# A new start for a one-core adaLN, attention and SwiGLU kernel: transfers in program order, TensorE on constants at first, eight heads of q without the shift of h

## The chip, the cores and the metric

The kernel runs on one core of a Trainium2 chip. The metric is device time in microseconds (us), lower is better. Each number is the median of several executions.

## The reference, cut to what matters

```python
mod = silu(c) @ w_mod                       # six vectors of 1024: sa, ca, ga, sb, cb, gb
h = layernorm(x) * (1 + ca) + sa            # x: 2048 rows of 1024
q = h @ wq                                  # 32 heads of 128
p = softmax(q @ k.T / sqrt(128))            # the last 512 keys; 4 key heads, each for 8 query heads
x = x + ga * ((p @ v) @ wo)
h = layernorm(x) * (1 + cb) + sb
x = x + gb * ((silu(h @ w_gate) * (h @ w_up)) @ w_down)     # 3584 wide
```

All inputs are bf16. For the change one identity matters: q = (n·(1+ca)) @ wq + sa @ wq, with n the normalised x. The second term is one column of 128 values per head, the same for every row of x.

## The kernel before

Rows go in four blocks of 512. Attention is a loop of 128 steps, one head of one block per step; q runs three heads ahead. Then comes the feed-forward part. Every weight comes through one transfer queue (SyncE's), and a scheduler decides the order of instructions on each engine. The parts that the change touches, cut:

```python
for tt in range(QT): load_x(tt)
for half in range(DH):
    load_wm(1, half); load_wm(0, half)      # w_mod columns: ca, then sa, 1 MB each
    load_wq(0, 0, (half,))
... # kT by transposing transfer, v, wq of heads 4-7
for half in range(DH):                      # start of the first block
    mod_cols(1, half, ca1, True)            # 32 matmuls of one column each
    mod_cols(0, half, sa, False)
    for dt in range(4 * half, 4 * half + 4):
        ln_affine(("h1", 0), dt, h0_ps[half][:, dt % 4, :], ca1, sa, dt % 2 == 0)
    ... # q of three heads, half of the sum
at(g + 2, load_rb, g); at(g + 4, emit_norm, g)      # softmax sums of four heads, back from DRAM
at(max(0, 4*hg - 3 + 2*i + j), bound_wq, hg, i, j)  # squares of wq for a bound: 32 x 1.23 us of DVE
for k in range(NU + 1):                             # the loop over heads
    if k % 4 == 2 and k + 6 < NU: load_wq((k + 6) // H, ((k + 6) % H) // 4)
    if k < NU: emit_s(k)                            # scores, exp, sums
    if k + LEAD < NU: emit_q(k + LEAD)              # LEAD = 3
    run_tasks(k)
    if k >= 1: ... emit_o(k - 1)
```

## Time and profile before

| | before |
|---|---|
| time, median of 4 executions | 1294.5 us |
| span of the profiled execution | 1293.1 us |
| TensorE (PE) busy | 99% |
| useful matmul time, counted as below | 1253.7 us |
| lost | 39.4 us |

The Trainium skill ("Trainium Kernel Development and Optimization", Performance Expectations) calls matmul busy time "a bad metric" for the distance to the best, because matmuls are pipelined. PE is 99% busy, and that hides where the time went. I therefore count weight loads (PEld), one for each matmul. Each load of a 128x512 matmul that has started counts 216 ns (215.8 unrounded), the spacing of such matmuls in the trace; narrower ones count in proportion; the l_ps and row_ps matmuls, of which four run side by side, count a quarter. Transposes, modulation, bias and warm-up matmuls count nothing. The loss at a time t is t less what was counted by then.

The table of windows of the kernel before (stretch, its length, then busy us and instructions of each engine, granted clock as a share, mean busy share of the transfer engines, GB/s):

```profile
core 0: us, PE busy (x) PEld busy (x) DVE busy (x) ACT busy (x) POOL busy (x), PEclk, DMA share, GB/s
10.00:20.00 10.00, 9.26 (x103) 5.90 (x104) 3.57 (x12) 3.18 (x5) 0.00 (x0) 1.00 1.17 378
20.00:30.00 10.00, 9.25 (x88) 4.60 (x87) 4.31 (x12) 2.77 (x4) 0.00 (x0) 0.83 1.02 254
40.00:60.00 20.00, 20.00 (x109) 8.48 (x108) 20.00 (x37) 14.55 (x21) 0.00 (x0) 1.00 0.71 221
60.00:80.00 20.00, 18.58 (x87) 7.79 (x86) 20.00 (x64) 14.29 (x20) 0.00 (x0) 1.00 1.02 300
80.00:100.00 20.00, 20.00 (x108) 8.64 (x106) 20.00 (x36) 8.13 (x12) 0.00 (x0) 1.00 1.00 334
```

The start is full of transfers (378 GB/s from 10 to 20 us). From 40 to 100 us the vector engine (DVE) is busy all the time, and between 60 and 80 us PE got only 87 matmuls. The timeline of PE at the start and around 77 us (start, length, engine, line, operation, tiles, count; in brackets the idle time before and what ended it):

```profile
15.44 2.72 PE L878 MATMUL q_ps<-hT,wq 128*128 128x512 bf16 x6 [0.44 <-ACT hT L826]
20.19 0.87 PE L728 MATMUL mod_ps<-siluc,wm_1_117 128*128 128x1 bf16 x29
21.31 0.94 PE L728 MATMUL mod_ps<-siluc,wm_1_119 128*128 128x1 bf16 x32 [0.25 <-DVE modT L730]
22.50 1.23 PE L953 MATMUL q_ps<-hT,wq 128*128 128x512 bf16 x4 [0.25 <-DVE modT L730]
23.53 4.27 PE L878 MATMUL q_ps<-hT,wq 128*128 128x512 bf16 x12
...
75.13 0.38 PE L983 MATMUL l_ps<-psB,ones_bf 128*32 128x512 bf16 x1 [0.91 <-DVE psB L975]
76.12 2.38 DVE L1004 TENSOR_TENSOR oT<-oT,rb 128x1024 bf16<-128x1024 bf16 x2
77.42 0.61 PE L1031 MATMUL a_ps<-wo,oT 128*128 128x512 bf16 x2 [0.51 <-DVE oT L1004]
```

Six q matmuls took 2.72 us, twelve took 4.27 us: most of these stood 427 ns apart, half rate. (The window of 10 to 20 us shows a clock of 1.00 all the same: the trace's first clock record starts at 19.8 us, and the view counts time without a record as full.) The clock fell again at 23.2 us. At 75 to 78 us PE waits for DVE.

### The profile page before, as it was taken

Reading aid. Unit: us, or ns where it says so; the run is one execution under the profiler, and the core shown is the slowest. Engines: PE = TensorE matmul, PEld = TensorE weight load, DVE = VectorE, ACT = ScalarE, POOL = GpSimd, SP = SyncE. Lnnn points to the kernel's source line nnn. Section 1 sums busy time; section 2 is a strip of 40 time slices with the busy share of each in tenths; the row PEclk is TensorE's granted clock in tenths of the full one; section 3 lists DMA queues with packets and bytes.
Section 4 is the critical chain, followed back from the end, with each engine's and each line's share of the span. In section 5 each row is a group of like instructions: output and inputs, shape, how many; then the busy total and the mean of one; then the engine's idle time right before and its main releaser. Section 6 shows DMA issues by size and latency. Waiting matters only on the chain.

```text
span 1293.1 us, 15465 instructions
## 1 busy us (share of the span) xinstructions
PE 1274.6 (99%) x6169; PEld 575.1 (44%) x6169; DVE 653.4 (51%) x1144; ACT 454.0 (35%) x646; POOL 0.7 (0%) x6
## 2 busy tenths in 40 slices
PE   6999999999999999999999999999999999999998
PEld 3444444444444444444444444444444444444444
DVE  5999768975569655597654641221222211222122
ACT  3755545655455555555453441001100111011100
POOL 0000000000000000000000000000000000000000
PEclk9999999999999999999999999999999999999999
DMA  9897584665354645355447475453536445454402
GB/s 303 273 320 215 206 203 144 187 172 177 122 184 137 180 139 172 130 156 171 163 137 232 161 224 180 145 191 131 165 105 215 167 144 180 137 191 131 147 18 83
DMA packets 219939, 221.08 MB, mean 171 GB/s; under 512 B 45385, under 2 KB 205129, under 8 KB 219858
## 3 DMA queue, kind: packets, MB, share of 16 engines
q1 hardware_dynamic: 214690, 215.54, 52.6%
q10 hardware_dynamic: 5168, 4.46, 1.0%
q8 instruction: 50, 0.82, 0.2%
q14 instruction: 31, 0.25, 0.1%
HBM read 207.63 MB, written 4.47 MB: 164 GB/s over the span
## 4 chain that ended last, share of the span: by engine, by line
PE 93%; DVE 4%; DMA 1%; issue 1%; ACT 0%; SPq 0%; DVEq 0%
PE gu_ps L1099 30%; PE a_ps L1031 17%; PE d_ps L1119 15%; PE q_ps L953 15%; PE o_ps L1014 8%; PE s_ps L966 7%; DVE junk L893 1%; PE l_ps L983 1%; PE q_ps L878 1%; DVE psA L973 1%; DVE qT L855 1%; DMA rb<-r_d 1%; DVE st L793 0%; DMA hT<-xn 0%; DVE psB L975 0%
## 5 line engine op out<-in xcount | busy, mean ns | idle before, releaser
L968 ACT ACTIVATE pT<-s_ps 128x1024 bf16<-128x1024 f32 x256 | 249.0, 1028 | 8.7 <-PE s_ps L966 5.3
L1031 PE MATMUL a_ps<-wo,oT 128*128 128x512 bf16 x1024 | 242.3, 379 | 1.7 <-DVE qT L855 1.2
L953 PE MATMUL q_ps<-hT,wq 128*128 128x512 bf16 x1000 | 237.1, 380 | 0.3 <-DVE modT L730 0.3
L1104 ACT ACTIVATE sg<-gu_ps 128x512 bf16<-128x512 f32 x112 | 66.9, 597 | 460.4 <-PE gu_ps L1099 306.6
L1105 DVE TENSOR_TENSOR guT<-gu_ps,sg 128x512 bf16<-128x512 f32 x112 | 77.5, 692 | 280.8 <-ACT sg L1104 280.8
L1099 PE MATMUL gu_ps<-hT,wu 128*128 128x512 bf16 x896 | 211.8, 379 | 0.0
L1099 PE MATMUL gu_ps<-hT,wg 128*128 128x512 bf16 x896 | 211.7, 379 | 0.0
L1119 PE MATMUL d_ps<-wd,guT 128*128 128x512 bf16 (+2 forms) x952 | 194.2, 367 | 0.0
L1031 PEld LDWEIGHTS <-oT 128*128 128x128 bf16 x1024 | 99.6, 98 | 123.8 <-issue 2.8
L1016 ACT CAST oT<-o_ps 128x512 bf16<-128x512 f32 x128 | 74.3, 580 | 226.3 <-PE o_ps L1014 226.3
L953 PEld LDWEIGHTS <-wq 128*128 128x128 bf16 x1000 | 97.6, 98 | 118.3 <-issue 0.3
L1119 PEld LDWEIGHTS <-guT 128*128 128x128 bf16 x952 | 90.7, 98 | 103.1
L1099 PEld LDWEIGHTS <-wg 128*128 128x128 bf16 x896 | 87.5, 98 | 105.8
L1099 PEld LDWEIGHTS <-wu 128*128 128x128 bf16 x896 | 87.4, 98 | 106.0 <-DMA wu<-in_B_w_up_dram 0.4
L966 PE MATMUL s_ps<-qT,kT 128*128 128x512 bf16 x512 | 131.8, 379 | 0.6 <-ACT pT L968 0.6
L1014 PE MATMUL o_ps<-pT,v_sb 128*128 128x512 bf16 x512 | 131.8, 380 | 0.0
L973 DVE TENSOR_TENSOR psA<-pT 128x1024 bf16<-128x1024 bf16 x128 | 88.2, 689 | 72.5 <-ACT pT L968 72.3
L855 DVE CAST qT<-q_ps 128x512 bf16<-128x512 f32 x128 | 87.8, 688 | 52.9 <-PE q_ps L953 50.7
L1004 DVE TENSOR_TENSOR oT<-oT,rb 128x1024 bf16<-128x1024 bf16 x64 | 78.0, 1223 | 20.6 <-DMA rb<-r_d 20.5
L966 PEld LDWEIGHTS <-kT 128*128 128x128 bf16 x512 | 50.0, 98 | 61.5 <-issue 1.3
L1014 PEld LDWEIGHTS <-v_sb 128*128 128x128 bf16 x512 | 47.3, 98 | 61.7 <-issue 9.0
L975 DVE TENSOR_TENSOR psB<-psA 128x512 bf16<-128x512 bf16 x128 | 53.8, 421 | 0.6
(267 smaller groups left out, 454.2 us busy)
## 6 DMA issues: line engine op xcount, KB each, us to landing
wq<-in_A_wq_dram SPq DMA_DIRECT2D x64, 512.0 KB
rb<-r_d SPq DMA_DIRECT2D x64, 512.0 KB
wo<-in_A_wo_dram SPq DMA_DIRECT2D x64, 512.0 KB
wg<-in_B_w_gate_dram SPq DMA_DIRECT2D x56, 512.0 KB
wu<-in_B_w_up_dram SPq DMA_DIRECT2D x56, 512.0 KB
wd<-in_B_w_down_dram SPq DMA_DIRECT2D x56, 512.0 KB
wmr<-in_w_mod_dram SPq DMA_DIRECT2D x8, 1024.0 KB
out_dram<-o_sb ACTq DMA_DIRECT2D x31, 128.0 KB
```

The source lines that it names most:

```text
L855: nc.vector.tensor_copy(out=t, in_=q_ps)
L953: nc.tensor.matmul(q_ps, lhsT=wq_tiles[(cc, h // 4, dt // 4)][:, dt % 4, (h % 4) * P:(h % 4 + 1) * P], rhs=hT[("h1", cc)][:, dt, :], start ...
L966: nc.tensor.matmul(s_ps[:, i, :], lhsT=kT[:, kv, j * P:(j + 1) * P], rhs=qT[g], start=True, stop=True)
L968: nc.scalar.activation(out=p[:, 2 * jj:2 * jj + 2, :], in_=s_ps, func=ACT.Exp, scale=scale)
L973: nc.vector.tensor_tensor(out=a, in0=p[:, 0:2, :], in1=p[:, 2:4, :], op=ALU.add)
L1004: nc.vector.tensor_tensor(out=oo, in0=oo, in1=rb, op=ALU.mult)
L1014: nc.tensor.matmul(o_ps, lhsT=v_sb[:, kv, j, :], rhs=pT[g][:, j, :], start=(j == 0), stop=(j == WT - 1))
L1016: nc.scalar.copy(out=oT[(cc, hg)][:, hi, :], in_=o_ps)
L1031: nc.tensor.matmul(a_ps, lhsT=oT[(cc, 2 * q + i)][:, hh % 4, t * P:(t + 1) * P], rhs=wo_tiles[(cc, q, dh, i)][:, hh % 4, :], start=(hh == ...
L1099: nc.tensor.matmul(ps[:, n, :], lhsT=gu_w[(cc, fg, nm, dt // 4)][:, dt % 4, fi * P:(fi + 1) * P], rhs=hT[("h2", cc)][:, dt, :], start=(dt ...
L1105: nc.vector.tensor_tensor(out=guT[(cc, fg)][:, fi, :], in0=ps[:, 1, :], in1=g, op=ALU.mult)
L1119: nc.tensor.matmul(d_ps, lhsT=guT[(cc, f // 4)][:, f % 4, t * P:(t + 1) * P], rhs=wd_tiles[(cc, dh, f // 4)][:, f % 4, c0:c0 + w], start=( ...
```

## The change

It means to start q sooner, to keep the array at full clock, and to take DVE's load out of the crowded stretch. Heads 0 to 7 of the first block are multiplied with h that has its scale but not its shift; the shift's part of w_mod (2 MB) is loaded later, behind the keys, and sa @ wq is added per head. In the loop, transfers and many DVE instructions are pinned to program order. The diff, cut to its core:

```diff
+    def pin(ins, what="steps"):                 # what: "dma" or "steps"
+        return tc.keep_in_program_order(ins) if stage[what] else ins
+    def fetch(out, in_):
+        pin(nc.sync.dma_start(out=out, in_=in_), "dma")
     for half in range(DH):
         load_wm(1, half)
-        load_wm(0, half)
         load_wq(0, 0, (half,))
+    load_wq(0, 1)
     kT = ...
+    for half in range(DH):
+        load_wm(0, half)
     v_sb = ...
-    load_wq(0, 1)
+    load_wq(0, 2)
+    warm(16)                                    # matmuls on constants; warm(2) after each row tile
-        mod_cols(0, half, sa, False)
-            ln_affine(("h1", 0), dt, ..., ca1, sa, dt % 2 == 0)
+            ... hT = h_ps * ca1                 # no shift
+    for g in range(LEAD0):                      # LEAD0 = 8 heads
+        ... put_stage(g, q_ps)                  # q to SBUF in fp32
+    for half in range(DH):
+        mod_cols(0, half, sa, False)
+    sa2 = ...                                   # sa as two bf16 columns
+    for g in range(LEAD0):
+        for dt in range(DT):
+            nc.tensor.matmul(b_ps[:, g, :], lhsT=wq_cols(0, g, dt), rhs=sa2[:, dt, :], ...)
+    ... qT[g] = q + bq[g];  hT += sa
     # loop
-        if k % 4 == 2 and k + 6 < NU: load_wq(...)          # both blocks of a group
+        if k > 3 and k % 4 >= 2 and 4 * (k // 4) + 8 < NU:
+            ... load_wq(g // H, (g % H) // 4, (k % 4 - 2,)) # one block per step
-        if k + LEAD < NU: emit_q(k + LEAD)
+        if k < 10: a q at even k only, of head 8 + k // 2;  then as before
-                at(max(0, 4*hg - 3 + 2*i + j), bound_wq, ...)
+                at((1 + hg % 3) * H + max(0, 4*hg - 3 + 2*i + j), bound_wq, ...)
-        plan_ln((cc + 1) * H + 12, ("h2", cc), cb1, sb)
+        plan = plan_ln if cc < NTC - 1 else plan_late_ln    # last block: rstd on DVE, rows in a batch
+        plan((cc + 1) * H + 13, ("h2", cc), cb1, sb)
... # wo and w_mod row blocks spread over steps; early oT copies on DVE; key sums moved to the last block
```

More of the change, by code (lines that the diff above doesn't have):

```diff
@@ L653, in big, with load @@
         return psp.tile(list(shape), dt, name=name, tag="s", bufs=2)
-    def load(out, in_, eng=None):
+    stage = {"dma": True, "steps": False}
+    def pin(ins, what="steps"):
+        return tc.keep_in_program_order(ins) if stage[what] else ins
+    def fetch(out, in_):
+        pin(nc.sync.dma_start(out=out, in_=in_), "dma")
+    def load(out, in_):
         with nc.allow_non_contiguous_dma(reason="weight slice"):
-            (eng or nc.sync).dma_start(out=out, in_=in_)
+            fetch(out=out, in_=in_)
     nc.scalar.preload_act_table_set("natural_log_exp_and_others")
@@ L666, in load_x @@
     def load_x(tt):
-        nc.sync.dma_start(out=xt[tt], in_=x2d[tt * P:(tt + 1) * P, :])
+        fetch(out=xt[tt], in_=x2d[tt * P:(tt + 1) * P, :])
     wm_tiles = {}
@@ L687, in fast_path @@
         load_wm(1, half)
-        load_wm(0, half)
         load_wq(0, 0, (half,))
+    load_wq(0, 1)
     kT = blkB("kT", [P, Hkv, W])
     for kv in range(Hkv):
-        nc.sync.dma_start_transpose(out=kT[:, kv, :], in_=A_k_cache[0, kv, k0:k0 + W, :])
+        pin(nc.sync.dma_start_transpose(
+            out=kT[:, kv, :], in_=A_k_cache[0, kv, k0:k0 + W, :]), "dma")
+    for half in range(DH):
+        load_wm(0, half)
     v_sb = blkB("v_sb", [P, Hkv, WT, Dh])
@@ L704, in fast_path, with warm @@
     nc.vector.memset(eps_t, eps)
+    warm_w = const.tile([P, 512], BF16, name="warm_w")
+    nc.gpsimd.memset(warm_w, 0.5)
+    warm_ps = mm("warm_ps")
+    def warm(n):
+        for _ in range(n):
+            tc.keep_in_program_order(
+                nc.tensor.matmul(warm_ps, lhsT=ones_bf, rhs=warm_w, start=True, stop=True))
+    warm(16)
     modT = const.tile([P, 4, DT], FP32, name="modT")
@@ L742, in fast_path, with load_rows @@
     row_d = {}
-    def load_rows(vecs, part):
-        wm_rows.append([])
-        for vec in vecs:
-            t = hpool.tile([P, 4, D], BF16, name="wmr", tag="hT")
-            load(t, wm_v[:, 4 * part:4 * part + 4, vec * D:(vec + 1) * D])
-            wm_rows[-1].append(t)
+    def load_rows(vec, part):
+        t = hpool.tile([P, 4, D], BF16, name="wmr", tag="hT")
+        load(t, wm_v[:, 4 * part:4 * part + 4, vec * D:(vec + 1) * D])
+        wm_rows.append(t)
     def mod_rows(n, part):
         ps = mm("row_ps")
-        tiles = wm_rows.pop()
+        tiles = [wm_rows.pop(0) for _ in range(2)]
         for k in range(4):
@@ L766, in mod_rows @@
             d = dp.tile([4, TCW], FP32, name="row_d", tag="row_d", bufs=2)
-            nc.sync.dma_start(out=d, in_=r[0:P:32, :])
+            fetch(out=d, in_=r[0:P:32, :])
             row_d[n] = d
     def load_gate(n, k, dst):
-        nc.sync.dma_start(out=dst.rearrange("p (a b) -> p a b", a=2),
+        fetch(out=dst.rearrange("p (a b) -> p a b", a=2),
                           in_=row_d[n][k:k + 2, :].partition_broadcast(P))
@@ L776, in load_cols @@
         with nc.allow_non_contiguous_dma(reason="1024 values to columns"):
-            nc.sync.dma_start(out=dst, in_=src)
+            fetch(out=dst, in_=src)
         if add_one:
@@ L788, in fast_path, with ln_stats @@
     ln = {}
-    def ln_stats(tt):
+    def ln_stats(tt, late=None):
         st = sm.tile([P, DH, nc.vector.BN_STATS_DIM], FP32, name="st", tag="st")
         for i in range(DH):
-            nc.vector.bn_stats(out=st[:, i, :], in_=xt[tt][:, i * 512:(i + 1) * 512])
+            pin(nc.vector.bn_stats(out=st[:, i, :], in_=xt[tt][:, i * 512:(i + 1) * 512]))
+        if late is not None:
+            nc.vector.bn_aggr(out=late[:, 0:2], in_=st)
+            return
         mv = sm.tile([P, 4], FP32, name="mv", tag="mv", bufs=4)
@@ L808, in ln_norm @@
         else:
-            nc.vector.tensor_scalar(out=n, in0=xt[tt], scalar1=mv[:, 0:1], scalar2=mv[:, 2:3],
-                                    op0=ALU.subtract, op1=ALU.mult)
+            pin(nc.vector.tensor_scalar(out=n, in0=xt[tt], scalar1=mv[:, 0:1],
+                                        scalar2=mv[:, 2:3], op0=ALU.subtract, op1=ALU.mult))
         return n
@@ L821, in ln_xpose @@
             new_hT(key)
-        nc.sync.dma_start_transpose(out=hT[key][:, :, t * P:(t + 1) * P], in_=xn.pop(tt))
+        pin(nc.sync.dma_start_transpose(
+            out=hT[key][:, :, t * P:(t + 1) * P], in_=xn.pop(tt)), "dma")
     def ln_affine(key, dt, ps, sc, sh, on_act):
@@ L828, in ln_affine @@
         else:
-            nc.vector.tensor_scalar(out=hT[key][:, dt, :], in0=ps, scalar1=sc[:, dt:dt + 1],
-                                    scalar2=sh[:, dt:dt + 1], op0=ALU.mult, op1=ALU.add)
+            pin(nc.vector.tensor_scalar(out=hT[key][:, dt, :], in0=ps, scalar1=sc[:, dt:dt + 1],
+                                        scalar2=sh[:, dt:dt + 1], op0=ALU.mult, op1=ALU.add))
     def ln_mod(key, dt, sc, sh):
@@ L836, in new_hT, with late_rstd, late_stats, plan_late_ln @@
         hT[key] = hpool.tile([P, DT, TCW], BF16, name="hT", tag="hT")
+    mvl = const.tile([P, QT, 4], FP32, name="mvl")
+    def late_rstd():
+        v, y, w = (mvl[:, :, i] for i in (1, 2, 3))
+        pin(nc.vector.tensor_scalar(out=v, in0=v, scalar1=eps, scalar2=None, op0=ALU.add))
+        nc.vector.tensor_scalar(out=y.bitcast(I32), in0=v.bitcast(I32), scalar1=1, scalar2=None,
+                                op0=ALU.logical_shift_right)
+        nc.vector.tensor_scalar(out=y.bitcast(I32), in0=y.bitcast(I32), scalar1=-1.0,
+                                scalar2=float(0x5f3759df), op0=ALU.mult, op1=ALU.add)
+        for _ in range(4):
+            nc.vector.tensor_tensor(out=w, in0=y, in1=y, op=ALU.mult)
+            nc.vector.scalar_tensor_tensor(out=w, in0=w, scalar=-0.5, in1=v, op0=ALU.mult,
+                                           op1=ALU.mult)
+            nc.vector.scalar_tensor_tensor(out=y, in0=w, scalar=1.5, in1=y, op0=ALU.add,
+                                           op1=ALU.mult)
+        for t in range(QT):
+            ln[S // P - QT + t] = mvl[:, t, :]
+    def late_stats(tt):
+        ln_stats(tt, mvl[:, tt % QT, :])
+    def plan_late_ln(k, key, sc, sh):
+        for t in range(QT):
+            tt = key[1] * QT + t
+            at(k + 2 * t, late_stats, tt)
+            at(k + 10 + 2 * t, ln_rows, tt)
+            at(k + 11 + 2 * t, ln_xpose, key, tt)
+        at(k + 8, late_rstd)
+        for dt in range(DT):
+            at(k + 24 + dt, ln_mod, key, dt, sc, sh)
     def plan_ln(k, key, sc, sh):
@@ L850, in fast_path @@
     LEAD = 3
+    LEAD0 = 8
     qT = {}
@@ L856, in put_q, with wq_cols @@
         qT[g] = t
-    new_hT(("h1", 0))
+    def wq_cols(cc, h, dt):
+        return wq_tiles[(cc, h // 4, dt // 4)][:, dt % 4, (h % 4) * P:(h % 4 + 1) * P]
+    h1 = ("h1", 0)
+    new_hT(h1)
     h0_ps = [big("h0_ps", (P, 4, TCW), BF16) for _ in range(2)]
@@ L867, in fast_path, with put_stage @@
                                 n[:, dt * P:(dt + 1) * P], ident)
+        warm(2)
+    stage_q = [blkC("q_f32", [P, 2, TCW], FP32) for _ in range(LEAD0 // 2)]
+    def put_stage(g, q_ps):
+        dst = stage_q[g // 2][:, g % 2, :]
+        if g % 2 == 0:
+            nc.scalar.copy(out=dst, in_=q_ps)
+        else:
+            nc.vector.tensor_copy(out=dst, in_=q_ps)
     q0_ps = []
@@ L870, in fast_path @@
         mod_cols(1, half, ca1, True)
-        mod_cols(0, half, sa, False)
         for dt in range(4 * half, 4 * half + 4):
-            ln_affine(("h1", 0), dt, h0_ps[half][:, dt % 4, :], ca1, sa, dt % 2 == 0)
+            src = h0_ps[half][:, dt % 4, :]
+            if dt % 2 == 0:
+                nc.scalar.activation(out=hT[h1][:, dt, :], in_=src, func=ACT.Copy,
+                                     scale=ca1[:, dt:dt + 1])
+            else:
+                nc.vector.tensor_scalar(out=hT[h1][:, dt, :], in0=src, scalar1=ca1[:, dt:dt + 1],
+                                        scalar2=None, op0=ALU.mult)
         if half == 0:
@@ L877, in fast_path @@
             dt, g = (4 * half + n // LEAD, n % LEAD) if half == 0 else (4 + n % 4, n // 4)
-            nc.tensor.matmul(q0_ps[g],
-                             lhsT=wq_tiles[(0, 0, dt // 4)][:, dt % 4, g * P:(g + 1) * P],
-                             rhs=hT[("h1", 0)][:, dt, :], start=(dt == 0), stop=(dt == DT - 1))
-    for g in range(LEAD):
-        put_q(g, q0_ps[g])
+            nc.tensor.matmul(q0_ps[g], lhsT=wq_cols(0, g, dt), rhs=hT[h1][:, dt, :],
+                             start=(dt == 0), stop=(dt == DT - 1))
+    for g in range(LEAD0):
+        if g >= LEAD:
+            q0_ps.append(mm("q_ps"))
+            for dt in range(DT):
+                nc.tensor.matmul(q0_ps[g], lhsT=wq_cols(0, g, dt), rhs=hT[h1][:, dt, :],
+                                 start=(dt == 0), stop=(dt == DT - 1))
+        put_stage(g, q0_ps[g])
+    for half in range(DH):
+        mod_cols(0, half, sa, False)
+    sa2 = const.tile([P, DT, 2], BF16, name="sa2")
+    nc.vector.tensor_copy(out=sa2[:, :, 0], in_=sa)
+    nc.vector.tensor_tensor(out=sa2[:, :, 1], in0=sa, in1=sa2[:, :, 0], op=ALU.subtract)
+    b_ps = mm("b_ps", (P, LEAD0, 2))
+    for g in range(LEAD0):
+        for dt in range(DT):
+            nc.tensor.matmul(b_ps[:, g, :], lhsT=wq_cols(0, g, dt), rhs=sa2[:, dt, :],
+                             start=(dt == 0), stop=(dt == DT - 1))
+    bq = const.tile([P, LEAD0], FP32, name="bq")
+    nc.vector.tensor_reduce(out=bq, in_=b_ps, axis=AX.X, op=ALU.add)
+    qs = [blkC("q_bf", [P, 4, TCW]) for _ in range(LEAD0 // 4)]
+    for g in range(LEAD0):
+        qT[g] = qs[g // 4][:, g % 4, :]
+        nc.vector.tensor_scalar(out=qT[g], in0=stage_q[g // 2][:, g % 2, :],
+                                scalar1=bq[:, g:g + 1], scalar2=None, op0=ALU.add)
+    for dt in range(DT):
+        nc.vector.tensor_scalar(out=hT[h1][:, dt, :], in0=hT[h1][:, dt, :],
+                                scalar1=sa[:, dt:dt + 1], scalar2=None, op0=ALU.add)
     k_ld = []
@@ L889, in bound_wq @@
     def bound_wq(hg, i, j):
-        w = wq_tiles[(0, hg, i)][:, 2 * j:2 * j + 2, :]
+        w = wq_tiles[(1 + hg % (NTC - 1), hg, i)][:, 2 * j:2 * j + 2, :]
         junk = wk.tile([P, 2, 512], BF16, name="junk", tag="psA", bufs=2)
         col = (hg * 2 + i) * 2 + j
-        nc.vector.scalar_tensor_tensor(out=junk, in0=w, scalar=1.0, in1=w, op0=ALU.mult,
-                                       op1=ALU.mult, accum_out=sq[:, col:col + 1])
+        pin(nc.vector.scalar_tensor_tensor(out=junk, in0=w, scalar=1.0, in1=w, op0=ALU.mult,
+                                           op1=ALU.mult, accum_out=sq[:, col:col + 1]))
     def load_k():
@@ L899, in load_k, with bound_k, bound_mod @@
             load(k_ld[0][:, kv], k_v[:, kv])
-    def bound_k():
-        kk = sm.tile([P, Hkv * WT], FP32, name="kk", tag="kk", bufs=1)
-        for i in range(Hkv * WT):
+    kk = const.tile([P, Hkv * WT], FP32, name="kk")
+    def bound_k(kv):
+        for j in range(WT):
+            i = kv * WT + j
             junk = wk.tile([P, Dh], BF16, name="junk", tag="psA", bufs=2)
-            src = k_ld[0][:, i // WT, i % WT, :]
-            nc.vector.scalar_tensor_tensor(out=junk, in0=src, scalar=1.0, in1=src, op0=ALU.mult,
-                                           op1=ALU.mult, accum_out=kk[:, i:i + 1])
+            src = k_ld[0][:, kv, j, :]
+            pin(nc.vector.scalar_tensor_tensor(out=junk, in0=src, scalar=1.0, in1=src,
+                                               op0=ALU.mult, op1=ALU.mult,
+                                               accum_out=kk[:, i:i + 1]))
+    def bound_mod():
         nc.vector.tensor_reduce(out=gd[:, 1:2], in_=kk, axis=AX.X, op=ALU.max)
@@ L919, in bound_final @@
         d = dp.tile([P, 4], FP32, name="gd_d", tag="gd_d", bufs=1)
-        nc.sync.dma_start(out=d, in_=gd)
+        fetch(out=d, in_=gd)
         row = wk.tile([1, P, 4], FP32, name="gd_row", tag="f32", bufs=2)
-        nc.sync.dma_start(out=row, in_=d)
+        fetch(out=row, in_=d)
         r = sm.tile([1, 8], FP32, name="gdr", tag="gdr", bufs=1)
@@ L953, in emit_q @@
             nc.tensor.matmul(q_ps,
-                             lhsT=wq_tiles[(cc, h // 4, dt // 4)][:, dt % 4,
-                                                                 (h % 4) * P:(h % 4 + 1) * P],
+                             lhsT=wq_cols(cc, h, dt),
                              rhs=hT[("h1", cc)][:, dt, :], start=(dt == 0), stop=(dt == DT - 1))
@@ L996, in load_rb @@
             rb = wk.tile([P, 2, TCW], FP32, name="rb", tag="rb", bufs=2)
-            nc.sync.dma_start(out=rb, in_=d[2 * i:2 * i + 2, :].partition_broadcast(P))
+            fetch(out=rb, in_=d[2 * i:2 * i + 2, :].partition_broadcast(P))
             rinv[g // 4].append(rb)
@@ L1003, in emit_norm @@
             oo = o[:, 2 * i:2 * i + 2, :]
-            nc.vector.tensor_tensor(out=oo, in0=oo, in1=rb, op=ALU.mult)
+            pin(nc.vector.tensor_tensor(out=oo, in0=oo, in1=rb, op=ALU.mult))
     def emit_o(g):
@@ L1015, in emit_o, with load_wo @@
                              start=(j == 0), stop=(j == WT - 1))
-        nc.scalar.copy(out=oT[(cc, hg)][:, hi, :], in_=o_ps)
+        if g < 2 * (LEAD0 - LEAD):
+            nc.vector.tensor_copy(out=oT[(cc, hg)][:, hi, :], in_=o_ps)
+        else:
+            nc.scalar.copy(out=oT[(cc, hg)][:, hi, :], in_=o_ps)
         del pT[g]
-    def load_wo(cc, q, dh):
-        for i in range(2):
-            t = blkC("wo", [P, 4, 512])
-            load(t, wo_v[:, q * HQ + 4 * i:q * HQ + 4 * i + 4, dh * 512:(dh + 1) * 512])
-            wo_tiles[(cc, q, dh, i)] = t
+    def load_wo(cc, q, dh, i):
+        t = blkC("wo", [P, 4, 512])
+        load(t, wo_v[:, q * HQ + 4 * i:q * HQ + 4 * i + 4, dh * 512:(dh + 1) * 512])
+        wo_tiles[(cc, q, dh, i)] = t
     def emit_wo(cc, q, u):
@@ L1050, in fast_path @@
         for part in range(2):
-            k = 16 * n + 8 * part + 1
-            at(k, load_rows, vecs, part)
-            at(k + 4, mod_rows, n, part)
+            k = 16 * n + 8 * part
+            at(k, load_rows, vecs[0], part)
+            at(k + 2, load_rows, vecs[1], part)
+            at(k + 5, mod_rows, n, part)
         at(16 * n + 15, load_gate, n, 0, gb_bc if n else ga_bc)
@@ L1061, in fast_path @@
             for j in range(2):
-                at(max(0, 4 * hg - 3 + 2 * i + j), bound_wq, hg, i, j)
-    at(6, load_k)
-    at(10, bound_k)
-    at(H + 2, bound_final)
+                at((1 + hg % (NTC - 1)) * H + max(0, 4 * hg - 3 + 2 * i + j), bound_wq, hg, i, j)
+    at(NU - H + 2, load_k)
+    for kv in range(Hkv):
+        at(NU - H + 20 + 2 * kv, bound_k, kv)
+    at(NU - H + 29, bound_mod)
+    at(NU + 3, bound_final)
     for g in range(3, NU, 4):
@@ L1072, in fast_path @@
         for q in range(NQ):
-            s0 = cc * H + q * HQ + HQ + 4
+            s0 = cc * H + q * HQ + HQ + 5
             for dh in range(DH):
-                at(s0 + 4 * dh - 4, load_wo, cc, q, dh)
+                for i in range(2):
+                    at(s0 + 4 * dh - 5 + i, load_wo, cc, q, dh, i)
             for u in range(2 * QT):
                 at(s0 + u, emit_wo, cc, q, u)
-        plan_ln((cc + 1) * H + 12, ("h2", cc), cb1, sb)
+        plan = plan_ln if cc < NTC - 1 else plan_late_ln
+        plan((cc + 1) * H + 13, ("h2", cc), cb1, sb)
     guT = {}
@@ L1131, in run_tasks @@
             f(*a)
+    stage["steps"] = True
     for k in range(NU + 1):
-        if k % 4 == 2 and k + 6 < NU:
-            load_wq((k + 6) // H, ((k + 6) % H) // 4)
+        if k > 3 and k % 4 >= 2 and 4 * (k // 4) + 8 < NU:
+            g = 4 * (k // 4) + 8
+            load_wq(g // H, (g % H) // 4, (k % 4 - 2,))
         if k < NU:
             emit_s(k)
-        if k + LEAD < NU:
+        if k < 2 * (LEAD0 - LEAD):
+            if k % 2 == 0:
+                emit_q(LEAD0 + k // 2)
+        elif k + LEAD < NU:
             emit_q(k + LEAD)
@@ L1146, in fast_path @@
             emit_o(k - 1)
+    stage.update(dma=False, steps=False)
     for cc in range(NTC):
```

## The prediction

> **What bounds it.** TensorE. The page gives PE 99% busy, but matmul ends are modelled, so I go by starts of matmuls in the timeline: consecutive 128x512 matmuls start 216 ns apart. At that rate the useful matmuls of the 1293.1 us span sum to about 1254 us; 39 us are lost. Lost: 22.5 us before 35 us, about 6 us between 60 and 250 us (1 us per 100 us recurs in attention, around l_ps), nothing in the feed-forward part (700 to 1280 us), and 5.4 us after the last matmul starts. Only the first item and some 3 us of the second can be won.
>
> **The start now.** DMA moves about 385 GB/s for the first 20 us (table of slices, windows). The first q matmuls start at 15.4 us; the second half of q waits for the last w_mod block (mod_ps to 22.3 us). Twelve q matmuls at 15.4 to 19.7 us and eight at 23.1 to 26.5 us start 427 ns apart, half rate: about 4 us. The Trainium skill, "TensorE: Matmul & The Clock Gate", Part 1, says the array runs at half clock until a window of about 3.4 us was busy, and falls back after an idle one; the trace agrees (full rate from 19.8, half from 23.2, full for good from 26.6 us). DVE is 100% busy from 40 to 100 us (windows); PE stalls 0.9 us at 76.5 us.
>
> **What the change does.**
> 1. h without its shift needs 1 MB x, 2 MB w_mod, 1 MB wq instead of 6 MB: at 385 GB/s both halves are there at about 15 us, not 20 us. But the transposes of normalised x end at 14.7 us, and the eight scalings of hT (0.78 ACT, 0.54 DVE, in turn) take 5 us: q runs from 15.4 us. 64 matmuls of 8 heads: 13.8 us at full rate, to about 29 to 32 us.
> 2. Warm-up matmuls (24, in idle time) save up to 3 to 4 us of half rate. I expect part of it: from 8 to 15 us PE has little to do.
> 3. Added on the path after q: shift columns (64 x 32 ns = 2 us), 64 bias matmuls of two columns (2 us, estimate from the same 32 ns), reduce, first q add: scores start at 32 to 36 us (28.1 now), with 64 instead of 30 q matmuls done. Lost by then: 18 to 22 us, against 22.
> 4. The first ten steps hold one q per two steps: PE 2.6 us a step, ACT 2.1 to 2.4 us (two exps of 1.03), DVE about 2.7 us (psA 0.69, psB 0.42, oT copy 0.69, half a q add, norms), plus eight hT adds of 0.41. A loss of 1 to 3 us here.
> 5. bound_wq (39 us of DVE) leaves the crowded first 100 us: most of the 3 us of stalls at 60 to 200 us goes. Pinned transfers: neutral.
> 6. Late LN on DVE, later bounds: off the path.
>
> **Prediction.** 4 us at the start plus 3 us from DVE relief: 1289 us, 8 in 10 between 1281 and 1297. Faster by over 2%: 0.01; within 2%: 0.97; slower: 0.02.
>
> **What would show it.** q dense at 216 ns from about 16 us; scores at 32 to 36 us; DVE below 100% at 40 to 100 us; no PE gap at 76 us; feed-forward and tail unchanged.
>
> **What would make it wrong.** The clock staying at half rate through 8 heads (5 us or more); the bias chain leaving PE idle over 3.4 us, so that it goes cold again; DVE becoming the limit of steps 0 to 10; a pinned transfer waiting for a buffer and holding up weights behind it.

## The result, and the profile after

The changed kernel took 1297.16 us (median of 4, 1297.01 to 1298.17); the kernel before took 1294.53 us (1292.82 to 1296.79). The ratio is 1.0021, 95% interval 1.0001 to 1.0041. Ratios here and below compare runs of the same rounds, so they are not quite the ratios of the medians. The sign is wrong and the time lies just above the stated range of 1281 to 1297 us.

The loss by stretch, counted in both traces:

```
us               0-30  30-40  40-60  60-100  100-300  300-700  700-800  800-end   sum
before          21.80   0.50   0.57   2.66     3.81     4.16     0.07     5.78   39.35
after           17.27   6.33   1.01   4.17     2.73     4.38     1.15     5.66   42.69
difference      -4.53  +5.83  +0.44  +1.51    -1.08    +0.22    +1.08    -0.12   +3.34
```

The first 30 us won 4.5 us, as planned. The next ten lost more than that. Then 60 to 100 us lost 1.5 us where a gain was expected, and the feed-forward part lost 1.1 us at one place. Windows after the change:

```profile
20.00:30.00 10.00, 9.87 (x45) 4.47 (x46) 3.40 (x8) 3.25 (x6) 0.00 (x0) 1.00 1.09 289
30.00:40.00 10.00, 8.64 (x145) 5.20 (x145) 6.83 (x23) 2.40 (x3) 0.00 (x0) 0.83 0.56 185
60.00:80.00 20.00, 18.81 (x88) 7.50 (x88) 18.12 (x30) 15.27 (x21) 0.00 (x0) 1.00 1.01 320
80.00:100.00 20.00, 18.42 (x94) 8.34 (x96) 13.40 (x25) 8.46 (x14) 0.00 (x0) 1.00 1.03 268
```

DVE is indeed relieved (13.40 us busy of 20 at 80 to 100 us, against 20.00), yet PE did not gain: 88 and 94 matmuls against 87 and 108. PE's timeline at the start:

```profile
23.41 7.93 PE L967 MATMUL q_ps<-hT,wq 128*128 128x512 bf16 x36
31.40 0.94 PE L753 MATMUL mod_ps<-siluc,wm_0_128 128*128 128x1 bf16 x32
32.20 0.94 PE L753 MATMUL mod_ps<-siluc,wm_1_130 128*128 128x1 bf16 x32
34.08 1.75 PE L979 MATMUL b_ps<-sa_502,wq 128*128 128x2 bf16 x64 [0.93 <-DVE sa_502 L975]
35.91 0.81 PE L1067 MATMUL q_ps<-hT,wq 128*128 128x512 bf16 x3
36.75 1.87 PE L1079 MATMUL s_ps<-q_bf,kT 128*128 128x512 bf16 x4
```

Thirty-six q matmuls in 7.93 us: full rate, as hoped. But then comes a chain that nothing hides: shift columns, a gap (0.93 us by the modelled end of the matmul before, 1.1 us from start to start), bias matmuls. After it four score matmuls took 1.87 us where 1.02 us is usual. The windows of that moment, and of what the transfers did next:

```profile
33.20:36.60 3.40, 2.45 (x67) 2.00 (x69) 2.86 (x13) 0.00 (x0) 0.00 (x0) 1.00 0.09 27
36.70:40.00 3.30, 3.00 (x8) 0.96 (x7) 3.00 (x8) 1.94 (x2) 0.00 (x0) 0.50 1.00 357
44.00:54.00 10.00, 9.86 (x59) 4.01 (x59) 6.72 (x13) 6.90 (x9) 0.00 (x0) 1.00 0.08 29
54.00:60.00 6.00, 5.95 (x28) 2.69 (x28) 4.52 (x9) 4.20 (x5) 0.00 (x0) 1.00 0.83 250
60.00:64.00 4.00, 3.17 (x17) 1.04 (x16) 3.97 (x6) 3.16 (x5) 0.00 (x0) 1.00 1.07 382
```

The clock was at one half from 36.6 to 40.0 us. From 44 to 54 us the transfer engines stood nearly idle (29 GB/s); then the held loads came together (250 GB/s, and 382 GB/s from 60 to 64 us). The queue's own waits tell why (what the queue waited for: us in total, times, longest). The first line is of the kernel before, the second of the changed kernel:

```profile
SPq L997 <- DMA r_d<-rinv: 123.2, 29, 6.8
```

```profile
SPq L664 <- DMA r_d<-rinv: 340.3, 30, 20.5
```

The pinned queue stood still from 37.6 to 53.9 us, until the softmax sums of four heads (r_d) were in DRAM, with weight blocks behind that load. PE then waited for those blocks:

```profile
61.58 1.04 PE L1067 MATMUL q_ps<-hT,wq 128*128 128x512 bf16 x4 [0.53 <-DMA wq<-in_A_wq_dram]
81.08 1.04 PE L779 MATMUL row_ps<-wmr,sil_183 128*32 128x512 bf16 x14 [1.30 <-DMA wmr<-in_w_mod_dram]
...
768.61 0.82 PE L1219 MATMUL gu_ps<-hT,wu 128*128 128x512 bf16 x3 [1.11 <-DMA wu<-in_B_w_up_dram]
```

### The profile page after: what moved, and what is told of

Read it like the earlier page. It is cut to its first block, busy times and chain, and to the rows that moved or that the text cites. A ratio compares the mean times of both kernels' runs of the same rounds, so it can differ in the third digit from the quotient of the medians.

```text
span 1296.4 us, 15465 instructions
## 1 busy us (share of the span) xinstructions
PE 1275.2 (98%) x6137; PEld 578.5 (45%) x6257; DVE 662.6 (51%) x1184; ACT 430.6 (33%) x619; POOL 1.2 (0%) x7
## 4 chain that ended last, share of the span: by engine, by line
PE 96%; DMA 2%; issue 1%; ACT 1%; DVE 1%
PE gu_ps L1219 30%; PE a_ps L1146 17%; PE q_ps L1067 15%; PE d_ps L1239 15%; PE o_ps L1127 8%; PE s_ps L1079 8%; DMA wq<-in_A_wq_dram 1%; PE l_ps L1096 1%; PE q_ps L967 1%; ACT pT L1081 0%; PE q_ps L961 0%; DMA wu<-in_B_w_up_dram 0%; DVE st L816 0%; PE row_ps L779 0%; DMA x_91<-in_A_x_dram 0%
## 5 line engine op out<-in xcount | busy, mean ns | idle before, releaser
L1081 ACT ACTIVATE pT<-s_ps 128x1024 bf16<-128x1024 f32 x256 | 251.7, 1027 | 86.4 <-PE s_ps L1079 84.1
L1067 PE MATMUL q_ps<-hT,wq 128*128 128x512 bf16 x904 | 224.5, 380 | 3.7 <-DMA wq<-in_A_wq_dram 1.0
L1067 PEld LDWEIGHTS <-wq 128*128 128x128 bf16 x960 | 93.6, 98 | 115.6 <-DMA wq<-in_A_wq_dram 2.8
L1079 PE MATMUL s_ps<-qT,kT 128*128 128x512 bf16 x480 | 123.8, 379 | 0.5 <-ACT pT L1081 0.3
L919 DVE CAST qT<-q_ps 128x512 bf16<-128x512 f32 x120 | 82.2, 685 | 76.8 <-PE q_ps L1067 76.8
L1132 ACT CAST oT<-o_ps 128x512 bf16<-128x512 f32 x118 | 68.5, 581 | 158.5 <-PE o_ps L1127 155.6
L1117 DVE TENSOR_TENSOR oT<-oT,rb 128x1024 bf16<-128x1024 bf16 x64 | 75.4, 1219 | 1.9 <-DMA rb<-r_d 1.8
```

Source lines behind the costliest of these rows:

```text
L919: nc.vector.tensor_copy(out=t, in_=q_ps)
L1067: nc.tensor.matmul(q_ps, lhsT=wq_cols(cc, h, dt), rhs=hT[("h1", cc)][:, dt, :], start=(dt == 0), stop=(dt == DT - 1))
L1079: nc.tensor.matmul(s_ps[:, i, :], lhsT=kT[:, kv, j * P:(j + 1) * P], rhs=qT[g], start=True, stop=True)
L1081: nc.scalar.activation(out=p[:, 2 * jj:2 * jj + 2, :], in_=s_ps, func=ACT.Exp, scale=scale)
L1117: pin(nc.vector.tensor_tensor(out=oo, in0=oo, in1=rb, op=ALU.mult))
L1132: nc.scalar.copy(out=oT[(cc, hg)][:, hi, :], in_=o_ps)
```

## The experiments

Fifteen kernels ran (there is no e4), all with correct results, each with five or six timed executions. Runs of one batch share their runs of the kernel before. The changed kernel itself was not timed again in the batches, which ran on three chips, so gains over it in the medians of single runs (e6, e7, e14) are not clear of noise and rest on the traces. That e16, which differs in the late layernorm alone, gave the same median in batch 4 speaks for the comparison. Theory A said that program order of the transfers costs the time, theory B that the detour of eight heads costs it.

### Batch 1: taking the change apart

**e1_loop_dma_free**: transfers free in the loop.

```diff
-    stage["steps"] = True
+    stage.update(dma=False, steps=True)
```

> The changed kernel, but transfers are held to program order only in the prologue, no longer in the attention loop. Theory A (transfers in program order cost): the waits of PE for wq, wmr and wu blocks between 60 and 84 us and at 768 us of the changed kernel (about 1.7 + 0.9 + 0.4 + 1.5 + 0.4 us, worked out from the gaps between weight loads) vanish, so 3 to 5 us less than the changed kernel, about 1293 us. Theory B (all of the loss is in the first 40 us, in the detour of eight heads): within 1 us of the changed kernel.

It took 1304.2 us, ratio to before 1.0062 (1.0046 to 1.0078): 7 us slower than the changed kernel. The stretch 40 to 60 us lost 9.9 us, because a wq block came late (PE's weight load at 47 us) and the array then ran at half clock from 45.5 to 52.3 us:

```profile
47.08 0.13 PEld L1067 LDWEIGHTS <-wq 128*128 128x128 bf16 x2 [7.53 <-DMA wq<-in_A_wq_dram]
```

Theory A falls in this form: left free, the scheduler's order is worse. Between 60 and 100 us, however, the loss was 1.15 us instead of 4.17 us, which points to the standing queue for those waits. (At 700 to 800 us it lost 3 us more.)

**e2_no_detour**: the changed kernel with the old start.

```diff
     for half in range(DH):
         load_wm(1, half)
+        load_wm(0, half)
         load_wq(0, 0, (half,))
-    ... eight heads, put_stage, b_ps, q + bq, hT += sa
+    ... the old start with ln_affine(ca1, sa) and three heads, warm(2) per row tile;
+        wq loads one group later, early oT copies back on ScalarE
-        if k < 10: a q at even k only
+        if k + LEAD < NU: emit_q(k + LEAD)
```

> The changed kernel with the old start: h with its shift at once, three heads ahead, the old order of the first loads; warm-up matmuls, pins and moved bounds stay. Theory B: the loss before 40 us falls from 23.6 us to 19 to 21 us (the old 22.3 less what a warm clock saves), so 2 to 4 us less than the changed kernel. Theory A: the start is not where the time went, so no more than 1 us less, as the waits of 60 to 84 us stay.

It took 1292.04 us, ratio 0.9971 (0.9955 to 0.9987). That is 5 us less than the changed kernel and faster than the kernel before. The detour is the loss, and it loses in two places: the loss at 40 us is 21.4 us instead of 23.6, and the stretch 60 to 100 us loses 0.7 us instead of 4.2. PE is without a gap there:

```profile
60.00:80.00 20.00, 20.00 (x108) 8.62 (x107) 15.41 (x27) 13.71 (x21) 0.00 (x0) 1.00 0.70 225
```

So theory B holds, but what I had put down to it alone (2 to 4 us in the first 40 us) is less than half of the 5 us. The queue is pinned in the same way here and waits for the same sums as long in all (338.0 us). But its first stand ends at 46.1 us instead of 53.9 us, and a step of the first ten holds a whole q here, so PE should need the blocks behind later. e6 and e10 below test whether the standing queue makes the waits of the changed kernel; why e2 escapes them was not tested by itself.

**e3_no_warm**: the changed kernel without matmuls on constants.

```diff
-    warm_ps = mm("warm_ps")
-    warm(16)
-        warm(2)
```

> The changed kernel without the warm-up matmuls. If they are worth what I think, the first 12 to 16 q matmuls start 427 ns apart instead of 216 ns and the kernel is 2.5 to 3.5 us slower than the changed one, about 1300 us. Rival: the clock would have risen anyway with the first dense window, and the loss at 30 us grows by less than 1 us.

It took 1298.12 us, ratio 1.0022 (1.0005 to 1.0038), the same ratio as the changed kernel's. The loss at 30 us was 18.1 us instead of 17.3. The rival fits: 0.9 us in this pair of traces, and nothing clear in the times. But the clock record of the changed kernel shows that the matmuls on constants had raised the clock by 5.9 us and that it fell again from 12.7 to 16.1 us, just before q. In e1 and e14, which have the same start up to 30 us, it did not fall there, and the loss at 30 us was 16.2 us, 1.9 us less than here. What the warm-up is worth differs from one execution to the next.

**e5_before_relief**: the kernel before, with the bound sums alone moved.

```diff
-                at(max(0, 4 * hg - 3 + 2 * i + j), bound_wq, hg, i, j)
+                at((1 + hg % (NTC - 1)) * H + max(0, 4 * hg - 3 + 2 * i + j), bound_wq, hg, i, j)
-    at(6, load_k); at(10, bound_k); at(H + 2, bound_final)
+    ... the same in the last block of rows
```

> The kernel before with the bound sums alone moved from the first 32 steps to later ones, as in the change. If DVE's crowding made the stalls at 75 to 79 us and 180 us (2.5 + 1.4 us), they go and the kernel is 2.5 to 4 us faster than before, about 1291 us. Rival: those stalls came from transfers or from the clock, and stay: within 1 us of before.

It took 1297.77 us, ratio 1.0013 (0.9998 to 1.0028): nothing won. DVE was no longer full, but its order was another. Up to 97 us it stood before an instruction whose transfer had not landed, with statistics, a sum and the q copy behind, on which PE's next bank depended. PE then waited 2 us, and the clock was at one half from 100.8 to 104.2 us:

```profile
97.28 0.17 DVE L779 TENSOR_SCALAR modT<-modT 128x8 f32<-128x8 f32 x1 [2.04 <-DMA modT<-row_d]
99.15 0.68 DVE L855 CAST qT<-q_ps 128x512 bf16<-128x512 f32 x1
99.89 0.38 PE L1035 MATMUL a_ps<-wo,oT 128*128 128x512 bf16 x1 [2.03 <-DVE qT L855]
```

The Trainium skill ("TensorE: Matmul & The Clock Gate", Architectural detail) says that ScalarE and VectorE are strictly first in, first out; this 2.04 us wait with ready work behind it agrees.

### Batch 2: mending the detour

**e6_wq_early**: in the changed kernel, one pair of loads goes ahead of the load that holds the queue.

```diff
+        if k < 2: load_wq(0, 3, (k,))
-        if k > 3 and k % 4 >= 2 and ...
+        if k > 7 and k % 4 >= 2 and ...
```

> The changed kernel with the two loads of wq for heads 12 to 15 moved from steps 6 and 7 to steps 0 and 1, ahead of the first load of the softmax sums (load_rb, step 5), behind which the transfer queue stood still from 37.6 to 53.9 us in the changed kernel. If the pinned queue is what made the waits of 60 to 84 us, the wait of 1.1 us before q at 61.6 us goes and those at 78 to 83 us shrink, as half a MB less stands in the rush after 54 us: 1 to 3 us less than the changed kernel. Rival: the rush is limited by bandwidth alone and the wait only moves to another block: within 1 us.

It took 1295.41 us, ratio 0.9995 (0.9981 to 1.0008), 1.75 us less by the medians. The stretch 60 to 100 us lost 2.45 us instead of 4.17, and the wait at 61 us is gone; one of 1.1 us before a wq block is left, at 79.7 us.

**e7_shift_early**: the shift's blocks are loaded before the keys, and its columns are computed before the last two of the eight heads.

```diff
+    for half in range(DH): load_wm(0, half)
     kT = ...
-    for half in range(DH): load_wm(0, half)
     for g in range(LEAD0):
+        if g == LEAD0 - 2:
+            ... mod_cols(0, half, sa, False); sa2 = ...
         ... q of head g
-    ... mod_cols(0, half, sa, False); sa2 = ...
     b_ps = ...
```

> The changed kernel with the shift's w_mod blocks loaded before the keys, and the shift columns computed before the last two of the eight heads, so that the chain from them to the bias matmuls is hidden behind two heads of q. Theory B1 (the exposed chain and the half clock that follows it cost the detour its gain): the 1.1 us gap before the bias matmuls goes, the clock stays at full rate after 36 us, the loss at 40 us falls from 23.6 to about 20 to 21 us, and the kernel is 2.5 to 4 us faster than the changed one. Theory B2 (the detour's loss lies in the later steps, 40 to 100 us): the loss at 40 us falls but is given back by 100 us, and the time stays within 1 us of the changed kernel.

It took 1294.9 us, ratio 0.9989 (0.9975 to 1.0003), 2.3 us less by the medians. The gap before the bias matmuls is gone and the clock holds. The first fence is PE's timeline in e7, the second its window after the bias matmuls:

```profile
28.12 1.74 PE L753 MATMUL mod_ps<-siluc,wm 128*128 128x1 bf16 x64
29.72 3.61 PE L974 MATMUL q_ps<-hT,wq 128*128 128x512 bf16 x16
33.17 1.74 PE L980 MATMUL b_ps<-sa,wq 128*128 128x2 bf16 x64
35.84 1.02 PE L1080 MATMUL s_ps<-q_bf,kT 128*128 128x512 bf16 x4
```

```profile
36.70:40.00 3.30, 2.62 (x13) 1.16 (x12) 3.30 (x8) 3.16 (x4) 0.00 (x0) 1.00 1.05 395
```

The loss at 40 us is 21.65 us (18.99 + 2.66) instead of 23.6, and it was not given back by 100 us. Theory B1 holds, a little under its 2.5 to 4 us.

**e8_no_detour_plain_ln**: e2 with the old layernorm of the last block of rows.

```diff
-        plan = plan_ln if cc < NTC - 1 else plan_late_ln
+        plan = plan_ln
```

> The changed kernel without the detour (as in the run e2_no_detour) and with the old layernorm of the last block of rows. In e2_no_detour four transposing transfers stand in a row before the next wu block, and PE waits 2.6 us for it at 763 us. If the late layernorm made that, the wait falls below 0.5 us and the kernel is 2 to 2.5 us faster than e2_no_detour, about 1289.5 us. Rival: the wait comes from the pinned order of transfers up to there and stays: within 1 us of e2_no_detour.

It took 1292.42 us, ratio 0.9974 (0.9960 to 0.9987), no faster than e2. The trace shows 0.72 us lost at 700 to 800 us instead of 2.44, but this execution also had a longer half-rate start (21.6 us lost by 30 us, against 20.7). The 2 us that I expected did not show in the times; this is inconclusive.

**e9_detour_mended**: e6, e7 and the old layernorm together (their three edits).

> The changed kernel with the detour kept and the mends of e6, e7 and the old layernorm together. If the three waits are independent, their gains add: 1 to 3, 2.5 to 4 and about 1.5 us, so about 1290 us, and the detour would be worth about as much as no detour. If the detour is a loss by its nature (more tensor work and a crowded transfer queue behind it), it stays above e8_no_detour_plain_ln by 2 us or more.

It took 1293.63 us, ratio 0.9985 (0.9971 to 0.9999). The gains add up to about 3.5 us of the 5 us. Between 60 and 100 us it still lost 2.2 us, at the next two weight blocks that stood behind the held queue.

### Batch 3: the rest of the detour, and what helps without it

**e10_detour_queue**: e9 with two more pairs of loads moved ahead.

```diff
+        if k in (6, 7): load_wq(0, 4, (k - 6,))
-        if k > 7 and k % 4 >= 2 and ...
+        if k > 11 and k % 4 >= 2 and ...
+            early = 4 if k == 8 else 0
-            at(k, load_rows, vecs[0], part); at(k + 2, load_rows, vecs[1], part)
+            at(k - early, load_rows, vecs[0], part); at(k + 2 - early, load_rows, vecs[1], part)
```

> e9_detour_mended with two more pairs of transfers moved ahead of the load that holds the queue: the wq blocks of heads 16 to 19 from steps 10 and 11 to 6 and 7, and the second pair of w_mod row blocks from steps 8 and 10 to 4 and 6. In e9 the transfer engines stood idle from 46 to 52 and 61 to 64 us, and PE then lost 2.1 us between 70 and 80 us on just these blocks. If the queue's standing still is the cause, that loss falls below 1 us, the kernel is 1 to 2 us faster than e9 (about 1292 us), and the detour is then no worse than no detour (1292 us). Rival: with bandwidth as the limit the wait moves to wo or x blocks; same time as e9 within 0.5 us.

It took 1292.41 us, ratio 0.9974 (0.9959 to 0.9989): 4.75 us less than the changed kernel by the medians, and level with no detour. The transfer engines no longer stand idle, and PE is nearly without gaps:

```profile
44.00:54.00 10.00, 9.77 (x59) 4.02 (x59) 7.27 (x14) 7.93 (x10) 0.00 (x0) 1.00 0.70 255
60.00:80.00 20.00, 19.89 (x107) 8.38 (x108) 18.76 (x34) 14.01 (x21) 0.00 (x0) 1.00 0.68 214
```

The waits of 60 to 84 us were therefore made by the standing queue, not by bandwidth.

**e11_no_detour_no_warm**: e8 without matmuls on constants (the edit of e3).

> e8_no_detour_plain_ln without the warm-up matmuls. If their worth is the half-rate matmuls at 15 to 27 us of the kernel before (about 4 us of loss), this is 1 to 3 us slower than e8, about 1294.5 us. Rival, from e3_no_warm, where taking them away cost the changed kernel under 1 us: within 1 us of e8.

It took 1293.04 us, ratio 0.9975 (0.9960 to 0.9990), within 1 us of e8. The rival fits again. At 30 us the loss was 22.0 us, against 20.5 to 21.6 us in the four kernels with this start and warm-up (e2, e8, e12, e13).

**e12_no_detour_no_relief**: e8 with the bound sums back in the first block.

```diff
-                at((1 + hg % (NTC - 1)) * H + max(0, ...), bound_wq, hg, i, j)
+                at(max(0, 4 * hg - 3 + 2 * i + j), bound_wq, hg, i, j)     # key sums likewise
```

> e8_no_detour_plain_ln with the bound sums back in the first 32 steps, where DVE was 100% busy in the kernel before. If the relief of DVE is what won the stalls of 60 to 200 us (before lost 5.3 us there, e8 1.9 us), they come back and the kernel is 2 to 4 us slower than e8, about 1295.5 us. Rival, from e5_before_relief, where the move alone won nothing: program order alone did it, and the time stays within 1 us of e8.

It took 1292.65 us, ratio 0.9985 (0.9969 to 1.0000); four executions lay at 1292.1 to 1292.9 us, two at 1295.5 and 1296.3. The trace lost 2.23 us between 60 and 100 us, against 0.50 in e8. So the relief of DVE is worth some 1.7 us in that stretch of one trace; over the whole span the two traces lost the same (37.1 and 37.0 us), and the times do not tell it apart from nothing.

**e13_no_detour_dma_free**: e8 with transfers free in the loop (the edit of e1).

> e8_no_detour_plain_ln with transfers free of program order in the loop. In e1_loop_dma_free the same edit put a wq block late and cost 7.6 us at 47 us. If the free order is what also spoilt e5_before_relief, this is 3 us or more slower than e8. Rival: the late block of e1 came from the detour's other load order, and here the time stays within 1 us of e8.

It took 1291.97 us, ratio 0.9972 (0.9958 to 0.9986), the lowest median of all. Without the detour it does not matter whether the loop's transfers are pinned. The late block of e1 belongs to the detour's other load order.

### Batch 4: what was still open

**e14_fill**: the changed kernel with matmuls on constants among the thin ones.

```diff
         mod_cols(0, half, sa, False)
+    warm(4)
     for g in range(LEAD0):
         ... eight bias matmuls
+        warm(1)
```

> The changed kernel with matmuls on constants put among the shift and bias matmuls: four in the gap of 1.1 us before the bias matmuls, one after each head's eight. They cost about 8 x 0.216 = 1.7 us of chain. If it is the thinness of these one- and two-column matmuls that let the clock fall, the trace shows no half-rate window near 36 us, the first score and q matmuls stand 216 ns apart, and about 1.9 us of loss there goes: the time is within 1 us of the changed kernel. Rival: the clock falls for another reason (the q phase ended, or a fixed period): the half-rate window stays and the kernel is 1.5 to 2 us slower than the changed one.

It took 1295.91 us, ratio 1.0000 (0.9986 to 1.0014), 1.25 us less by the medians. The half-rate window is gone. The first fence is PE's timeline in e14, the second the window:

```profile
31.94 1.02 PE L727 MATMUL warm_ps<-warm_w,ones_bf 128*128 128x512 bf16 x4
36.12 0.38 PE L727 MATMUL warm_ps<-warm_w,ones_bf 128*128 128x512 bf16 x1
37.12 1.02 PE L1083 MATMUL s_ps<-q_bf,kT 128*128 128x512 bf16 x4
```

```profile
36.70:40.00 3.30, 3.21 (x16) 1.29 (x14) 3.30 (x9) 2.25 (x3) 0.00 (x0) 1.00 1.05 392
```

So what let the clock fall was that this stretch held so little wide work; e14 filled both the gap and the thin matmuls, so it does not tell the two apart. The kernel before speaks for the thin matmuls: the clock fell at 23.2 us with no gap over 0.25 us. But gaps do it too: in e5 it fell at 100.8 us after one of 2.0 us, without thin matmuls. In the 3.4 us before each of these three falls (at 36.6, 23.2 and 100.8 us) the 512-column matmuls that started fill, at 216 ns each, about 1.3 us or less (an estimate from their starts). The filling costs what it saves: 6.33 us were lost from 30 to 40 us, as in the changed kernel. What this execution won in all (2.2 us of loss) lies before 30 us, where the clock did not fall, and after 60 us, which e14's edit does not explain.

**e15_no_detour_free**: e8 with nothing in the loop pinned.

```diff
-    stage["steps"] = True
+    stage.update(dma=False, steps=False)
```

> e13_no_detour_dma_free with the vector engine's instructions in the loop free too: nothing in the loop is held to program order, the bound sums stay moved. If it was the vector engine's order that spoilt e5_before_relief (there a qT copy stood behind an instruction that waited 2.0 us for a transfer), stalls of 2 us or more come back between 60 and 200 us and this is 2 to 4 us slower than e13. Rival: e5 was spoilt by the order of its prologue: within 1 us of e13.

It took 1306.46 us, ratio 1.0082 (1.0069 to 1.0096): 14 us more than e13, from which only the pins on DVE are missing. It lost 3.3 us from 60 to 100 us, 8.8 from 100 to 300 and 7.2 from 300 to 700. One of these places:

```profile
186.62 2.67 DVE L854 TENSOR_SCALAR hT<-hT,modT 128x512 bf16<-128x512 bf16 x8 [4.90 <-DMA hT<-xn]
190.55 2.79 PE L1024 MATMUL q_ps<-hT,wq 128*128 128x512 bf16 x7 [2.78 <-DVE qT L917]
```

DVE stood 4.9 us before an instruction that waited for a transfer, and PE waited for the q copies behind it. With free time on DVE, the scheduler places such instructions too early. The effect is larger than the 2 to 4 us that I expected.

**e16_plain_ln**: the changed kernel with the old layernorm of the last block (the edit of e8).

> The changed kernel with the old layernorm of the last block of rows alone. If the four transposing transfers in a row before the wu block made PE's wait of 1.7 us at 768 us, it falls below 0.5 us and the kernel is about 1 us faster than the changed one, 1296 us. Rival, from e8_no_detour_plain_ln, whose trace lost the wait but whose time did not move: no change over 0.5 us.

It took 1297.1 us, ratio 1.0005 (0.9991 to 1.0018), the median of the changed kernel. Its loss from 700 to 800 us stayed at 1.15 us; a gap of 1.3 us before a gate matmul stands there in place of the wait for wu. The rival was right, and what causes the loss at the start of the feed-forward part is not settled.

## Why the prediction was wrong

The reading of the kernel before held in the main. PE was the bound, only the start and some 3 us later could be won, and 2% was out of reach either way. The sum failed: "4 us at the start plus 3 us from DVE relief". In the traces, the start lost 1.3 us by 40 us instead of winning 4, the rest of attention up to 300 us lost 0.9 us instead of winning 3, and the stretch from 300 us on lost 1.2 us instead of nothing. Two steps failed, 3 and 5. Term by term:

- *Step 1, q earlier and dense, was right.* q ran at full rate from 16 us, and by 30 us the change had won 4.5 us.
- *Step 3, the added path, was mis-sized, and its worst part stood only among the risks.* I expected 18 to 22 us lost by the first scores at 32 to 36 us. They came at 36.8 us with 21.9 us lost: a little late, but within that loss. Then 1.8 us more were lost at half clock, 23.6 us by 40 us. The shift columns and the bias matmuls took 3.5 us, close to the 4 us of the estimate. The gap of 1.1 us before them and a full window at half clock after them (36.6 to 40.0 us, 0.50 granted) were not in the sum. e7 hid the chain and won 2.3 us; e14 filled it with wide matmuls and the clock stayed up. I had put the fall down as possible if PE idled over 3.4 us. (It did fall so in e1, at 45.5 us, where PE idled from 40 to 47 us.) Here PE idled 1.1 us, but 64 of the 67 matmuls of that window were two columns wide. The fall at 23.2 us in the kernel before, with PE busy for 2.9 of 3.4 us, could have warned me. (The Trainium skill, "TensorE: Matmul & The Clock Gate", Wait — 56ns, not 53.3ns?, gives a floor of about 25 ns from start to start for small matmuls. The trace agrees: 64 two-column matmuls in 1.75 us, with their weight loads. My 32 ns each were too high.)
- *Step 2, the warm-up, was too high.* "Part of" 3 to 4 us came to 0.9 us in the pair of traces (e3), 1.9 us against an execution whose clock stayed up (e14), and under 1 us in the medians, not clear of noise (e3, e11). The Trainium skill ("TensorE: Matmul & The Clock Gate", Part 1) describes a busy window of about 3.4 us that raises the clock. The trace agrees on the window (3.4 us at half rate from 12.7 to 16.1 us in the changed kernel, in spite of the warm-up). Without warm-up the first dense stretch of q raised the clock anyway, at 18.9 us (e3).
- *Step 5, 3 us from DVE relief and pinned transfers neutral, failed on both counts.* DVE was relieved as foreseen. But in the changed kernel the pinned queue stood still for the softmax sums (37.6 to 53.9 us), and the weights behind it came late: 4.2 us lost at 60 to 100 us instead of 2.7. e6 and e10 moved three pairs of loads ahead of the standing load, and the stretch fell to 1.15 us. Pinning is neutral without the detour (e13 against e8). With it the free order is worse still (e1) and the pinned order needs its loads placed by hand. The relief alone won nothing (e5), because DVE's free order then put waiting instructions in front. With DVE pinned it is worth about 1.7 us in one stretch of a trace, and nothing clear in the times (e12).
- *Step 4, 1 to 3 us lost in the first ten steps, was about right or high*: 0.4 us more than before at 40 to 60 us. But I did not see that shorter steps also need the weights sooner.
- *"Feed-forward unchanged" was wrong by 1.1 us*, at 768 us. Step 6 had put the late layernorm off the path; undoing it moved the wait and did not take it away (e16), so whether it is the cause stays open.

Could either kernel be beaten? Yes. e2, e8, e10 and e13 lie at 1292.0 to 1292.4 us, ratios 0.9971 to 0.9974 to the kernel before; they cannot be told apart. The detour, fully mended, is worth no more than no detour. All of what helped comes from the rest of the change, of which DVE's pinned order is the part that cannot be left out (e15).

What stays open: the 1.2 to 2 us at the start of the feed-forward part, and why e8's shorter wait there did not show in its times. The runs e2, e8, e12 and e13 share one prologue but lost 20.7, 21.6, 20.5 and 21.6 us by 30 us, with half-rate windows at different times after the start. The five executions with the changed kernel's start and warm-up show the same: 17.0 to 17.3 us where the clock fell at 12 to 13 us (changed kernel, e6, e16), 16.2 us where it did not (e1, e14). That the scatter of times comes from the place of these windows is likely, but was not tested.

## What to carry to other kernels

When work is taken out of the way to start earlier, add up the chain that has to be caught up later, and hide it behind dense work before the result is needed; thin matmuls on that chain can cost the clock besides. A transfer queue held in order stands still at its first unready load, so place loads that nothing holds back ahead of it, and check again when steps become shorter. Freeing an engine wins only if its order keeps instructions that wait for transfers out of the way of those that the bounding engine needs.

## What the Trainium skill lacked or had wrong

- "TensorE: Matmul & The Clock Gate" (Why this matters for your kernels) asks for no idle gaps over about 3 us to keep the full clock. Here that was not enough. The clock fell at 36.6 us with no gap over 1.1 us, after a window (33.2 to 36.6 us) that held mostly matmuls of two columns, and at 23.2 us in the kernel before with no gap over 0.25 us, after mostly one-column matmuls. Twelve 512-column matmuls among and before the bias ones kept it up (e14). The page does not say that thin matmuls count for little.
- No page that I found gives what a queue in program order costs the loads that stand behind one whose source is not ready (it would belong to "DMA: Bandwidth & Descriptors"): here it stood 16 us (37.6 to 53.9 us), at 29 GB/s from 44 to 54 us, and PE lost 4.2 us from 60 to 100 us, against 1.15 us with three pairs of loads moved ahead (e10).
